# Finer handover steps for the attention units, other steps for the v_m products, and the order of their splits

## The chip, the cores and the metric

The program runs on one core of a Trainium2 chip. The metric is device time in microseconds (us) of one execution of the whole program. Before the change it is 1615.07 us, the median of 3 runs (1614.37 to 1615.68).

## The reference

Three stages follow each other. q, k, v have shape (8 batches, 8 heads, 576 positions, 64), phi (8, 8, 576, 32).

```python
a = exp(phi - max(phi));  a = a / (sum(a) + 1e-9)          # over the 32 memory slots
k_m = einsum('bhsm,bhsd->bhmd', a, k);  v_m = einsum('bhsm,bhsd->bhmd', a, v)
s = (q @ k_m.T) / sqrt(64);  p = softmax(s)                # 32 scores for each position
x = (p @ v_m), heads side by side                          # 4608 x 512
h = x @ w_in;  h = max(0.01 * h, h);  x = h @ w_out         # 512 -> 2048 -> 512
y = (sigmoid(x @ w_gate) * (x @ w_val)) @ w2_out            # 512 -> 1536 -> 512
```

## The kernel before, in words

**Precision.** Large products run on two float32r numbers for each float32: a high part (`hi`, a copy rounded on ScalarE) and a low part (`lo`, the rest, subtracted on VectorE or GpSimd). `split` (L157) makes both: L158 the copy, L159 the subtraction. A product takes three matmuls: hi by hi, lo by hi, hi by lo.

**The first network.** p @ v_m @ w_in is computed as p @ (v_m @ w_in). `vw_pair` (L717) makes v_m @ w_in of a batch for two of its 8 column blocks: 32 matmuls into two PSUM banks, one for each group of 4 heads, and then four `split`s, from the banks into two of the nine slots of the tag vw. So a batch needs four pairs. `m1_in` (L738) multiplies it with the attention weights p (`at_hi`, `at_lo`) and puts the leaky ReLU through ScalarE (gr) and a `split` (gh, gl); `m1_out` (L761) multiplies with w_out into four PSUM banks (acc), and at the end of a half batch copies acc to obuf (L781).

**Steps.** The main loop counts steps i. Step i runs `m1_out` of one block of 128 hidden columns and half a batch (288 positions); a batch has 32 steps, its first half in the first 16, and batch b from 1 on has steps 32b to 32b + 31. In the code of one step the order is: the split of gr that belongs to step i + 1 (`fin`), `m1_in` of step i + 2 with its gr, then vector work (`run(vs)`, the generators taking turns operation by operation), TensorE work of the units (`ts_`), `vw_pair` where its step has come, `m1_out`, and loads. Every engine takes its instructions in this order, and so a step that waits holds what stands behind it on its engine.

**Units.** The attention of one batch and one group of 4 heads is a unit, cut into parts (`PARTS`, L688): v1 to v11 on VectorE, ScalarE and GpSimd, t1 to t8 on TensorE, lp, lk, lq the loads. `SCHED["chain"]` gives each part its step, counted from the unit's own start; for batches 3 to 7 the two units start at step 32(b-1) - 8 and 32(b-1) + 8, for batches 1 and 2 at `units`. Parts that matter here: v5 (L521) takes reciprocals on VectorE and scales the new k_m, v_m on ScalarE out of PSUM (tile e, L541); t5, v6 make their transposes (kvT); t8, v8 the scores, two PSUM banks, transposed into e (L592) by VectorE; v9 (L633) the maximum on VectorE (L638) and the subtraction (L640), v9e exp on ScalarE (L647), v10 (L650) sum, reciprocal on VectorE (L654 to L658) and the product with it (L660), v10t (L665) a transpose on VectorE (L676), v11 (L679) the split into at_hi and at_lo. From batch 2 on the subtractions of v9 and v11 and the product of v10 are on GpSimd (POOL). t1, t2, t4, t5, t8 and the pairs share two PSUM buffers (`psa`, L432).

**The weights of the second network** are converted in the steps from 31 on, in 36 pieces (`stash_jobs`, L253), one stage of a piece in each step. A piece begins as float32 bits; stage a (L182) has three conversions on ScalarE (y L186, k L187, raw L189), b (L192) a clip on VectorE, b2 a combination of y and raw on VectorE, c an addition on GpSimd. Sums of the pieces are split (hl, L290 and L296) and stored to memory (gvs) for later. The pieces of a gate and value block begin at steps 0 and 3 of twelve, counted from step 31, and their splits are in steps 8 to 12 of the twelve; w2 pieces begin three steps apart.

**After step 255** comes the second network, matmuls on TensorE with operands from memory.

Of the kernel before, what the change touches and what calls it, by code (L numbers as in the profile page):

```python
# [8 lines left out]
F32 = mybir.dt.float32  # L9
# [5 lines left out]
AX = mybir.AxisListType  # L15
# [27 lines left out]
           'v4': 5,  # L43
           't4': 6,
           'vq': 6,
           'v5': 7,
           't5': 9,
           'v6': 10,
# [6 lines left out]
           'v11': 17},  # L55
 'units': [1, 13, 30, 42],
 'unit': [-8, 8],
 'vw': [20, 22, 36, 38],
 'vw_last': [20, 22, 25, 28],
 'vw1': [26, 28, 31, 37],  # L60
 'vw2': [54, 57, 59, 63],
 'groups': [4,4,4,4],
 'chain1': {'lp': -9,
            'lk': -4,
# [26 lines left out]
def tile_kernel(  # L91
# [13 lines left out]
    nc = tc.nc  # L105
    P = 128
    B, H, S, D = q.shape
# [13 lines left out]
    VB = 256  # L121
# [15 lines left out]
    q, k, v, phi = (x.rearrange("b (h g) s d -> b g h s d", g=NG) for x in (q, k, v, phi))  # L137
# [13 lines left out]
    def f32(ap):  # L151
        return ap.bitcast(F32)
# [4 lines left out]
    def split(raw, hi, lo, eng=nc.vector):  # L157
        nc.scalar.copy(hi, raw)  # L158
        eng.tensor_sub(lo, raw, f32(hi))  # L159
# [7 lines left out]
    PC = 512  # L167

    class Piece:
        i = -1  # L170

        def __init__(self, src, done, f_dst=None, raw=None):
            self.src, self.done, self.f_dst, self.raw = src, done, f_dst, raw
# [8 lines left out]
        def a(self):  # L182
            w = self.raw.rearrange("p (n t) -> p n t", t=2)
            self.y = cvp.tile([P, PC], F32, tag="y", name="y", bufs=5)
            self.k = cvp.tile([P, PC], F32, tag="k", name="k", bufs=4)
            nc.scalar.activation(self.y, w[:, :, 1].bitcast(F32), AF.Abs, scale=2.0 ** -3)  # L186
            nc.scalar.activation(self.k, w[:, :, 0], AF.Copy, scale=2.0 ** -27, bias=2.0 ** 25)  # L187
            hi = w[:, :, 1]
            nc.scalar.activation(hi.bitcast(I32), hi.bitcast(F32), AF.Prelu, scale=2.0 ** -60, alpha=2.0 ** 120)  # L189
            yield  # L190

        def b(self):  # L192
            y = self.y
            nc.vector.tensor_scalar(y, y, 2.0 ** -18, 15359.998046875, op0=ALU.max, op1=ALU.min)
            yield

        def b2(self):
# [55 lines left out]
    def stash_jobs():  # L253
        held = {}

        def conv(src, done):
            p = Piece(src, None)

            def c():
                yield from p.c()  # L260
                done(p.f)

            return p, [p.a, p.b, p.b2, c]
# [68 lines left out]
        for th in range(NTH):  # L332
            for j in range(TH // 2):
                for i, w in enumerate((w_gate, w_val)):
                    for e in range(2):
# [3 lines left out]
                            lambda f, k=((th, j, i), e): held.update({k: f}),  # L339
# [20 lines left out]
    vw = {}  # L360
    un = {}
# [67 lines left out]
    def unit_engine(part, u):  # L429
        return nc.gpsimd if u[0] > 1 or f"{part}.{u[0] * NG + u[1]}" in SCHED["upool"] else nc.vector  # L430
# [37 lines left out]
    def etile(u):  # L468
        if u == FIRST2:
            return un[u]["m0"][:, 0:S].rearrange("p (a m) -> p a m", m=M)  # L470
        return ap_.tile([P, S // 32, M], F32, tag="e", name="e")
# [46 lines left out]
                p[:, 4 * D:4 * D + 2], s["t"].rearrange("p h m -> p (h m)"), ones[:, 0:2], start=True, stop=True  # L518
            )

    def v5(u):  # L521
        s = un[u]
        p = s.pop("p")
        r = ap_.tile([P, 4], F32, tag="r", name="r", bufs=2)
        nc.vector.tensor_scalar_add(r[:, 0:1], p[:, 4 * D:4 * D + 1], 1e-9)
        yield
        nc.vector.reciprocal(r[:, 0:1], r[:, 0:1])
        yield
        if u[0] == 0:
            nc.vector.tensor_scalar_mul(r, mask, r[:, 0:1])  # L530
            yield
        x = etile(u)
        x = s["x"] = x.rearrange("p a m -> p (a m)")[:, 0:4 * D].rearrange("p (a f) -> p a f", a=2)
        if u[0] == 0:
            for j in range(2):
                nc.scalar.activation(x[:, 0, j * D:(j + 1) * D], p[:, 0:D], AF.Copy, scale=r[:, j:j + 1])
            for j in range(2):
                m = 2 if j == u[1] else 3
                nc.scalar.activation(x[:, 1, j * D:(j + 1) * D], p[:, D:2 * D], AF.Copy, scale=r[:, m:m + 1])
        else:  # L540
            nc.scalar.activation(  # L541
                x.rearrange("p i (a d) -> p i a d", a=2),
                p[:, 0:2 * D].rearrange("p (i a d) -> p i a d", i=2, a=1).to_broadcast([P, 2, 2, D]),
                AF.Copy, scale=r[:, 0:1],
            )
        yield

    def t5(u):
        s = un[u]
# [80 lines left out]
        )  # L630
        yield

    def v9(u):  # L633
        s = un[u]
        sc = s["sc"]
        nb = S // 32
        st = s["st"] = ap_.tile([P, nb], F32, tag="st", name="st", bufs=2)
        nc.vector.reduce_max(st, sc, axis=AX.X)  # L638
        yield
        unit_engine("v9", u).tensor_sub(  # L640
            sc, sc, st.rearrange("p (a o) -> p a o", o=1).to_broadcast([P, nb, M])
        )
        yield

    def v9e(u):
        sc = un[u]["sc"]
        nc.scalar.activation(sc, sc, AF.Exp, scale=SCALE)  # L647
        yield

    def v10(u):  # L650
        s = un[u]
        sc, st = s["sc"], s["st"]
        nb = S // 32
        nc.vector.reduce_sum(st, sc, axis=AX.X)  # L654
        yield
        nc.vector.tensor_scalar_add(st, st, 1e-9)
        yield
        nc.vector.reciprocal(st, st)  # L658
        yield
        unit_engine("v10", u).tensor_mul(  # L660
            sc, sc, st.rearrange("p (a o) -> p a o", o=1).to_broadcast([P, nb, M])
        )
        yield

    def v10t(u):  # L665
        s = un[u]
# [12 lines left out]
    def v11(u):  # L679
# [7 lines left out]

    PARTS = {  # L688
        "v1": v1, "t1": t1, "v2": v2, "t2": t2, "v3": v3, "v3e": v3e, "v4": v4, "t4": t4, "v5": v5, "t5": t5,
        "v6": v6, "v9": v9, "v9e": v9e, "v10": v10, "v10t": v10t, "v11": v11,  # L690
        "vq": vq, "t8": t8_both, "v8": v8_both, "lp": unit_phi, "lk": unit_kv,
    }
    for h in range(HG):
# [23 lines left out]
    def vw_pair(b, j0):  # L717
        js = (j0, j0 + 1)
        ps = [psa("ps_vw") for _ in range(NG)]
        for n, j in enumerate(js):  # L720
            for h in range(HG):
                for g in range(NG):
                    nc.tensor.matmul(  # L723
                        ps[g][M * h:M * h + M, n * VB:(n + 1) * VB],
                        kvT[b, g][D * g:D * g + D, 1, M * h:M * h + M],
                        win[j][D * g:D * g + D, h, :], start=True, stop=True,
                    )
        for j in js:
            vw[b, j] = wtile("vw", [P, 2, NG, VB], F32R, "vw")
        for g in range(NG):  # L730
            for n, j in enumerate(js):
                split(ps[g][:, n * VB:(n + 1) * VB], vw[b, j][:, 0, g], vw[b, j][:, 1, g])

    hps = {}
    gt = {}
# [289 lines left out]
    with tc.manual_schedule():  # L1025
# [91 lines left out]
        def unit_parts(i):  # L1117
            vs, ts_, ls = [], [], []
            for u, u0 in U0.items():
                parts = [n for n, k in SCHED["chain1" if u[0] == 1 else "chain"].items() if k == i - u0]  # L1120
                v = [PARTS[n](u) for n in parts if n[0] == "v"]
                if v:
                    vs.append(chain(v))
                ts_ += [(PARTS[n], u) for n in parts if n[0] == "t"]
                ls += [
                    (PARTS[n], u) for n in parts
                    if n[0] == "l" and u not in units[:3]
                ]
            return vs, ts_, ls
# [166 lines left out]
```

## Time and profile before

| what | value |
|---|---|
| median of 3 runs | 1615.07 us |
| the profiled execution: its own time, its span | 1615.78 us, 1614.0 us |
| mean granted TensorE clock | 0.989 of full speed |
| VectorE, ScalarE, GpSimd busy | 833.8, 710.8, 433.9 us (52%, 44%, 27% of the span) |
| matmul instructions | 10544 |
| memory read, written | 219.68 MB, 47.19 MB |

The span is from the first to the last instruction. A busy engine is one that executes; register, wait and DMA-issuing instructions don't count. Matmuls overlap each other, so that single times of matmuls add up to more than the time they take.

### The profile page before, as it was taken

The numbers are of one execution on the slowest core, as the hardware profiler recorded it, in microseconds if no ns is written. First come the engines' busy times: TensorE is split into PE (matmuls) and PEld (weight loads), VectorE is DVE, ScalarE is ACT, GpSimd is POOL, SyncE is SP. The second block draws the span as 40 slices with busy tenths as digits, with TensorE's granted clock in tenths as the row PEclk, the third lists the DMA queues.
The fourth block names the chain that finished last, engine by engine and source line by source line (L and its number), as shares of the span: only waits on it lengthen the run. The fifth ranks groups of instructions, "written<-read, shape, count | busy, mean of one in ns | idle before, by whom it ended". The sixth has DMA issues, their size and how long they took to land.

```text
span 1614.0 us, 27349 instructions
## 1 busy us (share of the span) xinstructions
PE 1553.8 (96%) x10544; PEld 1358.4 (84%) x10544; DVE 833.8 (52%) x1426; ACT 710.8 (44%) x1602; POOL 433.9 (27%) x429
## 2 busy tenths in 40 slices
PE   4789999999999999999999999999999999999998
PEld 2677888999898899999988888888888888888898
DVE  6986444455545445523154474365544474355544
ACT  5885455565556555645333142222333143223332
POOL 3886343554445444543200020000200020000100
PEclk9799999999999999999999999999999999999999
DMA  9822543554555554412455456546556446436592
GB/s 302 276 52 68 154 142 101 153 177 120 159 161 172 152 149 130 138 42 93 172 196 187 141 168 221 194 133 201 193 181 208 143 158 227 165 116 221 219 396 77
DMA packets 203490, 268.66 MB, mean 166 GB/s; under 512 B 95072, under 2 KB 140128, under 8 KB 203360
## 3 DMA queue, kind: packets, MB, share of 16 engines
q1 hardware_dynamic: 203360, 266.92, 51.5%
q8 instruction: 83, 1.36, 0.3%
q14 instruction: 47, 0.39, 0.1%
HBM read 219.68 MB, written 47.19 MB: 165 GB/s over the span
## 4 chain that ended last, share of the span: by engine, by line
PE 61%; DMA 1%; DVE 0%; ACT 0%; POOL 0%; issue 0%; SPq 0%
PE oacc L978 18%; PE ps_y L880 14%; PE ps_x L880 9%; PE ps_z L880 9%; PE acc L772 7%; PE ps_h L750 3%; DMA wt<-gvs 1%; PE ps_vw L723 0%; PE ps_kv L515 0%; ACT gh L158 0%; PE ps_sc L582 0%; POOL e L640 0%; DVE vw L159 0%; DVE sums L277 0%; DVE st L654 0%
## 5 line engine op out<-in xcount | busy, mean ns | idle before, releaser
L772 PE MATMUL acc<-gh,wo 128*128 128x288 f32 x2048 | 429.3, 301 | 7.1 <-ACT obuf L781 3.9
L772 PEld LDWEIGHTS acc<-gh,wo 128*128 128x128 f32 x2048 | 328.4, 189 | 33.6 <-issue 14.0
L772 PE MATMUL acc<-gl,wo 128*128 128x288 f32 x1024 | 306.2, 299 | 6.4 <-POOL gl L159 6.4
L159 POOL TENSOR_TENSOR gl<-gr,gh 128x288 fp32r<-128x288 f32 x250 | 216.4, 870 | 342.0 <-ACT gh L158 247.6
L978 PE MATMUL oacc<-w2t,pt 128*128 128x512 f32 x1296 | 296.3, 389 | 0.0
L978 PEld LDWEIGHTS oacc<-w2t,pt 128*128 128x128 f32 x1296 | 243.1, 188 | 50.4
L880 PE MATMUL ps_y<-xo,wt 128*128 128x512 f32 (+1 forms) x1080 | 251.9, 369 | 0.0
L750 PE MATMUL ps_h<-at_hi,vw 128*128 128x288 f32 x1024 | 215.3, 299 | 6.1 <-ACT vw L158 4.7
L880 PEld LDWEIGHTS ps_y<-xo,wt 128*128 128x128 f32 x1080 | 190.3, 188 | 33.8
L843 POOL TENSOR_TENSOR xo<-xr,xo 128x512 fp32r<-128x512 f32 (+1 forms) x16 | 23.0, 1460 | 671.0 <-ACT xo L839 671.0
L772 PEld LDWEIGHTS acc<-gl,wo 128*128 128x128 f32 x1024 | 193.7, 189 | 10.4 <-POOL gl L159 10.2
L755 ACT ACTIVATE gr<-ps_h 128x288 f32<-128x288 f32 x256 | 105.6, 413 | 204.4 <-PE ps_h L750 175.4
L750 PEld LDWEIGHTS ps_h<-at_hi,vw 128*128 128x128 f32 x1024 | 167.3, 191 | 7.5 <-ACT vw L158 5.6
L880 PE MATMUL ps_z<-xo,wt 128*128 128x512 f32 (+1 forms) x720 | 167.4, 368 | 0.9 <-DMA wt<-gvs 0.9
L880 PE MATMUL ps_x<-xo,wt 128*128 128x512 f32 (+1 forms) x720 | 167.5, 368 | 0.0
L750 PE MATMUL ps_h<-at_lo,vw 128*128 128x288 f32 x512 | 152.1, 297 | 0.0
L915 ACT CAST pt<-sg 128x512 fp32r<-128x512 f32 (+1 forms) x120 | 69.4, 578 | 182.0 <-DVE sg L908 182.0
L880 PEld LDWEIGHTS ps_z<-xo,wt 128*128 128x128 f32 x720 | 127.0, 188 | 23.5 <-DVE pt L912 1.1
L880 PEld LDWEIGHTS ps_x<-xo,wt 128*128 128x128 f32 x720 | 127.2, 188 | 22.9
L158 ACT CAST gh<-gr 128x288 fp32r<-128x288 f32 x256 | 111.3, 435 | 2.5
L750 PEld LDWEIGHTS ps_h<-at_lo,vw 128*128 128x128 f32 x512 | 97.6, 191 | 0.0
L927 ACT COPY tmp<-ps_x 128x512 f32<-128x512 f32 (+1 forms) x60 | 32.5, 542 | 136.7 <-PE ps_x L880 136.7
(169 smaller groups left out, 1730.4 us busy)
## 6 DMA issues: line engine op xcount, KB each, us to landing
wt<-gvs SPq DMA_DIRECT2D x210, 512.0 KB, 4.5
w2t<-w2s SPq DMA_DIRECT2D x60, 512.0 KB, 5.4
gvs<-hl SPq DMA_DIRECT2D x84, 256.0 KB, 2.3
x2s<-obuf SPq DMA_DIRECT2D x15, 576.0 KB, 3.7
win<-in_moe_w_in_dram SPq DMA_DIRECT2D x16, 512.0 KB, 9.8
wo_bits<-in_moe_w_out_dram SPq DMA_DIRECT2D x16, 512.0 KB, 10.3
xr<-x2s SPq DMA_DIRECT2D x16, 512.0 KB, 6.6
out_dram<-osum SPq DMA_DIRECT2D x32, 256.0 KB, 2.0
```

Of the source, the lines that this page charges most:

```text
L158: nc.scalar.copy(hi, raw)
L159: eng.tensor_sub(lo, raw, f32(hi))
L750: nc.tensor.matmul(p[:, :HALF], w, x, start=(n == 0), stop=(n == 3 * NG - 1))
L755: nc.scalar.activation(gr, p[:, :HALF], AF.Prelu, alpha=0.01)
L772: nc.tensor.matmul(a[d][:, :HALF], w[:, ds_], x, start=(open_ and n == 0), stop=(close and n == 2),)
L843: eng.tensor_sub(t[:, 1, :h], x_operand(n, k, a), f32(t[:, 0, :h]))
L880: nc.tensor.matmul(bank, w[:, l, a, :], x[:, r, :h], start=(start and i == 0), stop=(i == 5), skip_group_check=not start,)
L915: nc.scalar.copy(d[:, 0, :h], s)
L927: read(lambda: nc.scalar.copy(s1, x))
L978: nc.tensor.matmul(bank[i], pt[2 * f + t][:, l, q * P:(q + 1) * P], w2t[f][:, r, :], start=(f == 0 and l + r == 0), stop=(f == TH - 1 and ...
```

## The change

The chain that was used for batches 2 to 7 stays for batch 2 under the name `chain2`. The chain for batches 3 to 7 cuts v5, v9 and v10 where the work goes from one engine to another: v5r (reciprocals) and v5x (scaling) at 7 and 8 instead of both at 7; v9m (maximum), v9s (subtraction) and v9e (exp) at 13, 14, 15 instead of all at 13; v10r (sum and reciprocal) and v10m (product) at 16 and 17 instead of 14; v10t at 18 instead of 15, v11 at 20 instead of 17. The pairs of batches 3 to 6 go from steps 20, 22, 36, 38 (from 32(b-1)) to 21, 28, 32, 37, those of batch 7 each one step later, and the last of batch 2 from 63 to 64. In `vw_pair`, all pairs, the two high parts of a bank are written first and then its two low parts. For the 36 pieces converted from step 31 on (`late`) the third conversion goes from stage a to stage b, behind the clip. The instructions themselves and their operands stay.

```diff
--- before.py
+++ after.py
@@ -29,6 +29,34 @@
  'gldve': [3, 4, 6, 12, 26, 31],
  'upool': ['v10.1', 'v10.2', 'v10.3', 'v11.0', 'v11.1', 'v11.2', 'v11.3', 'v9.0', 'v9.2', 'v9.3'],
  'chain': {'lp': -8,
...
+           'v5r': 7,
+           'v5x': 8,
+           't5': 9,
+           'v6': 10,
+           't8': 11,
+           'v8': 12,
+           'v9m': 13,
+           'v9s': 14,
+           'v9e': 15,
+           'v10r': 16,
+           'v10m': 17,
+           'v10t': 18,
+           'v11': 20},
+ 'chain2': {'lp': -8,
            'lk': -5,
            'lq0': -8,
            'lq1': -7,
@@ -55,10 +83,10 @@
            'v11': 17},
  'units': [1, 13, 30, 42],
  'unit': [-8, 8],
- 'vw': [20, 22, 36, 38],
- 'vw_last': [20, 22, 25, 28],
+ 'vw': [21, 28, 32, 37],
+ 'vw_last': [21, 23, 26, 29],
  'vw1': [26, 28, 31, 37],
- 'vw2': [54, 57, 59, 63],
+ 'vw2': [54, 57, 59, 64],
  'groups': [4,4,4,4],
  'chain1': {'lp': -9,
             'lk': -4,
@@ -167,7 +195,7 @@
     PC = 512
 
     class Piece:
-        i = -1
+        late = False
 
         def __init__(self, src, done, f_dst=None, raw=None):
             self.src, self.done, self.f_dst, self.raw = src, done, f_dst, raw
@@ -185,13 +213,19 @@
             self.k = cvp.tile([P, PC], F32, tag="k", name="k", bufs=4)
             nc.scalar.activation(self.y, w[:, :, 1].bitcast(F32), AF.Abs, scale=2.0 ** -3)
             nc.scalar.activation(self.k, w[:, :, 0], AF.Copy, scale=2.0 ** -27, bias=2.0 ** 25)
-            hi = w[:, :, 1]
+            if not self.late:
+                self.sign()
+            yield
+
+        def sign(self):
+            hi = self.raw.rearrange("p (n t) -> p n t", t=2)[:, :, 1]
             nc.scalar.activation(hi.bitcast(I32), hi.bitcast(F32), AF.Prelu, scale=2.0 ** -60, alpha=2.0 ** 120)
-            yield
 
         def b(self):
             y = self.y
             nc.vector.tensor_scalar(y, y, 2.0 ** -18, 15359.998046875, op0=ALU.max, op1=ALU.min)
+            if self.late:
+                self.sign()
             yield
 
         def b2(self):
@@ -255,6 +289,7 @@
 
         def conv(src, done):
             p = Piece(src, None)
+            p.late = True
 
             def c():
                 yield from p.c()
@@ -518,10 +553,10 @@
                 p[:, 4 * D:4 * D + 2], s["t"].rearrange("p h m -> p (h m)"), ones[:, 0:2], start=True, stop=True
             )
 
-    def v5(u):
-        s = un[u]
-        p = s.pop("p")
-        r = ap_.tile([P, 4], F32, tag="r", name="r", bufs=2)
+    def v5r(u):
+        s = un[u]
+        p = s["p"]
+        r = s["r"] = ap_.tile([P, 4], F32, tag="r", name="r", bufs=2)
         nc.vector.tensor_scalar_add(r[:, 0:1], p[:, 4 * D:4 * D + 1], 1e-9)
         yield
         nc.vector.reciprocal(r[:, 0:1], r[:, 0:1])
@@ -529,6 +564,10 @@
         if u[0] == 0:
             nc.vector.tensor_scalar_mul(r, mask, r[:, 0:1])
             yield
+
+    def v5x(u):
+        s = un[u]
+        p, r = s.pop("p"), s["r"]
         x = etile(u)
         x = s["x"] = x.rearrange("p a m -> p (a m)")[:, 0:4 * D].rearrange("p (a f) -> p a f", a=2)
         if u[0] == 0:
@@ -545,6 +584,10 @@
             )
         yield
 
+    def v5(u):
+        yield from v5r(u)
+        yield from v5x(u)
+
     def t5(u):
         s = un[u]
         p = s["p"] = psa("ps_kvT")
@@ -630,37 +673,53 @@
         )
         yield
 
-    def v9(u):
-        s = un[u]
-        sc = s["sc"]
+    def v9m(u):
+        s = un[u]
         nb = S // 32
         st = s["st"] = ap_.tile([P, nb], F32, tag="st", name="st", bufs=2)
-        nc.vector.reduce_max(st, sc, axis=AX.X)
-        yield
+        nc.vector.reduce_max(st, s["sc"], axis=AX.X)
+        yield
+
+    def v9s(u):
+        s = un[u]
+        sc, st = s["sc"], s["st"]
+        nb = S // 32
         unit_engine("v9", u).tensor_sub(
             sc, sc, st.rearrange("p (a o) -> p a o", o=1).to_broadcast([P, nb, M])
         )
         yield
 
+    def v9(u):
+        yield from v9m(u)
+        yield from v9s(u)
+
     def v9e(u):
         sc = un[u]["sc"]
         nc.scalar.activation(sc, sc, AF.Exp, scale=SCALE)
         yield
 
-    def v10(u):
+    def v10r(u):
+        s = un[u]
+        sc, st = s["sc"], s["st"]
+        nc.vector.reduce_sum(st, sc, axis=AX.X)
+        yield
+        nc.vector.tensor_scalar_add(st, st, 1e-9)
+        yield
+        nc.vector.reciprocal(st, st)
+        yield
+
+    def v10m(u):
         s = un[u]
         sc, st = s["sc"], s["st"]
         nb = S // 32
-        nc.vector.reduce_sum(st, sc, axis=AX.X)
-        yield
-        nc.vector.tensor_scalar_add(st, st, 1e-9)
-        yield
-        nc.vector.reciprocal(st, st)
-        yield
         unit_engine("v10", u).tensor_mul(
             sc, sc, st.rearrange("p (a o) -> p a o", o=1).to_broadcast([P, nb, M])
         )
         yield
+
+    def v10(u):
+        yield from v10r(u)
+        yield from v10m(u)
 
     def v10t(u):
         s = un[u]
@@ -687,7 +746,8 @@
 
     PARTS = {
         "v1": v1, "t1": t1, "v2": v2, "t2": t2, "v3": v3, "v3e": v3e, "v4": v4, "t4": t4, "v5": v5, "t5": t5,
-        "v6": v6, "v9": v9, "v9e": v9e, "v10": v10, "v10t": v10t, "v11": v11,
+        "v5r": v5r, "v5x": v5x, "v6": v6, "v9": v9, "v9m": v9m, "v9s": v9s, "v9e": v9e, "v10": v10, "v10r": v10r,
+        "v10m": v10m, "v10t": v10t, "v11": v11,
         "vq": vq, "t8": t8_both, "v8": v8_both, "lp": unit_phi, "lk": unit_kv,
     }
     for h in range(HG):
@@ -728,8 +788,11 @@
         for j in js:
             vw[b, j] = wtile("vw", [P, 2, NG, VB], F32R, "vw")
         for g in range(NG):
-            for n, j in enumerate(js):
-                split(ps[g][:, n * VB:(n + 1) * VB], vw[b, j][:, 0, g], vw[b, j][:, 1, g])
+            ws = [(ps[g][:, n * VB:(n + 1) * VB], vw[b, j]) for n, j in enumerate(js)]
+            for x, w in ws:
+                nc.scalar.copy(w[:, 0, g], x)
+            for x, w in ws:
+                nc.vector.tensor_sub(w[:, 1, g], x, f32(w[:, 0, g]))
 
     hps = {}
     gt = {}
@@ -1117,7 +1180,7 @@
         def unit_parts(i):
             vs, ts_, ls = [], [], []
             for u, u0 in U0.items():
-                parts = [n for n, k in SCHED["chain1" if u[0] == 1 else "chain"].items() if k == i - u0]
+                parts = [n for n, k in SCHED[{1: "chain1", 2: "chain2"}.get(u[0], "chain")].items() if k == i - u0]
                 v = [PARTS[n](u) for n in parts if n[0] == "v"]
                 if v:
                     vs.append(chain(v))
```

## Rows read from the trace of the kernel before

**Rows 1.** The page, part 1: busy us, share, instructions.
```profile
PE 1553.8 (96%) x10544; PEld 1358.4 (84%) x10544; DVE 833.8 (52%) x1426; ACT 710.8 (44%) x1602; POOL 433.9 (27%) x429
```

**Rows 2.** Stretches of undisturbed steps: from:to, us, busy by engine, clock, DMA.
```profile
721.47:791.07 69.60, 69.60 (x525) 69.60 (x523) 16.20 (x22) 31.75 (x77) 27.13 (x30) 1.00 0.38 131
274.42:277.57 3.15, 3.15 (x36) 2.52 (x35) 1.54 (x2) 1.31 (x4) 0.81 (x1) 1.00 0.88 232
371.59:375.09 3.50, 3.50 (x52) 2.80 (x50) 2.89 (x5) 1.54 (x5) 2.11 (x2) 1.00 0.46 123
```

**Rows 3.** Stretches of two steps, where v9 to v10t end.
```profile
280.07:286.03 5.96, 5.38 (x39) 4.90 (x37) 2.27 (x4) 3.44 (x8) 3.23 (x4) 1.00 1.02 320
...
655.43:661.03 5.60, 5.34 (x40) 5.03 (x39) 3.27 (x7) 4.25 (x11) 3.99 (x6) 1.00 0.56 187
```

**Rows 4.** Waits of TensorE, 266 to 715 us: total us, times, longest.
```profile
PE acc L772 <- POOL gl L159: 3.9, 10, 0.5
PE acc L772 <- ACT obuf L781: 2.0, 4, 0.7
PE ps_vw L723 <- DVE e L592: 1.7, 4, 0.6
PE acc L772 <- ACT gh L158: 1.4, 4, 0.7
```

**Rows 5.** Stretches of one step at the end of a half.
```profile
266.41:269.34 2.93, 2.70 (x25) 2.46 (x19) 1.50 (x4) 1.75 (x6) 0.00 (x0) 1.00 0.02 6
...
584.53:587.84 3.31, 2.57 (x20) 2.34 (x18) 0.73 (x2) 2.77 (x7) 0.00 (x0) 1.00 0.20 77
```

**Rows 6.** Order of time, ScalarE at step 127: start, us, instruction.
```profile
446.53 0.47 ACT L541 ACTIVATE e<-ps_kv,r 128x256 f32<-128x256 f32 x1
...
448.55 1.30 ACT L781 COPY obuf<-acc 128x288 f32<-128x288 f32 x4
```

**Rows 7.** Stretches of one step, a pair in the step of v8.
```profile
409.89:414.61 4.72, 4.24 (x58) 3.05 (x51) 2.26 (x6) 2.83 (x7) 0.81 (x1) 1.00 0.88 272
...
548.40:553.49 5.09, 4.32 (x58) 3.06 (x51) 2.26 (x6) 3.22 (x8) 0.81 (x1) 1.00 0.89 281
```

**Rows 8.** Stretches of one step, a pair in the step of v5.
```profile
179.31:183.92 4.61, 4.23 (x54) 3.06 (x50) 1.54 (x4) 0.78 (x2) 1.79 (x2) 1.00 0.27 46
261.81:266.41 4.60, 4.22 (x55) 3.04 (x51) 1.15 (x4) 1.07 (x3) 0.54 (x1) 1.00 0.00 0
```

**Rows 9.** Stretches of step 31, of step 57 and the one after.
```profile
163.60:168.14 4.54, 3.10 (x28) 2.73 (x21) 2.11 (x6) 3.47 (x10) 0.50 (x1) 1.00 0.01 4
235.47:244.84 9.37, 5.26 (x53) 3.24 (x51) 5.15 (x11) 3.83 (x8) 4.35 (x5) 0.87 0.18 61
244.84:249.42 4.58, 4.58 (x28) 4.58 (x21) 1.61 (x4) 1.73 (x5) 1.54 (x2) 0.52 0.32 108
```

**Rows 10.** Order of time, all engines at step 57; the idle time before in brackets.
```profile
239.46 0.41 ACT L158 CAST gh<-gr 128x288 fp32r<-128x288 f32 x1
...
240.75 1.16 POOL L660 TENSOR_TENSOR e<-e,st 128x576 f32<-128x576 f32 x1
...
242.95 1.96 PE L723 MATMUL ps_vw<-win,kvT 64*32 64x256 f32 x30 [4.11 <-DVE mx L457]
```

**Rows 11.** Order of time, ScalarE at step 163.
```profile
549.20 0.41 ACT L290 CAST hl<-sums 128x256 fp32r<-128x256 f32 x1 [2.97 <-DMA gvs<-hl]
```

**Rows 12.** Order of time, ScalarE: the copies of a pair.
```profile
415.57 0.36 ACT L158 CAST vw<-ps_vw 128x256 fp32r<-128x256 f32 x1
...
416.42 0.65 ACT L158 CAST vw<-ps_vw 128x256 fp32r<-128x256 f32 x2 [0.49 <-DVE vw L159]
...
417.62 0.37 ACT L158 CAST vw<-ps_vw 128x256 fp32r<-128x256 f32 x1 [0.55 <-DVE vw L159]
```

**Rows 13.** The tile raw: duration in ns (min/median/max), first and last start.
```profile
L189 ACT ACTIVATE raw<-raw x36: 648/669/701, 164.2 to 678.8; 128x512 int32<-128x512 f32 x36
```

**Rows 14.** A stretch after the gap of step 57.
```profile
243.00:249.00 6.00, 6.00 (x47) 4.78 (x48) 2.30 (x6) 1.73 (x5) 1.12 (x2) 0.50 0.28 87
```

More of the change, by code (lines that the diff above doesn't have):

```diff
@@ L45 @@
            'vq': 6,
+           'v5r': 7,
[12 more added lines that the diff above has]
+ 'chain2': {'lp': -8,
+           'lk': -5,
+           'lq0': -8,
+           'lq1': -7,
+           'lq2': -4,
+           'lq3': -3,
+           'v1': -5,
+           't1': 0,
+           'v2': 1,
+           't2': 2,
+           'v3': 3,
+           'v3e': 4,
+           'v4': 5,
+           't4': 6,
+           'vq': 6,
            'v5': 7,
@@ L648, in v9e @@
         yield
-    def v10(u):
+    def v10r(u):
         s = un[u]
         sc, st = s["sc"], s["st"]
-        nb = S // 32
         nc.vector.reduce_sum(st, sc, axis=AX.X)
@@ L659, in v10 @@
         yield
+    def v10m(u):
+        s = un[u]
+        sc, st = s["sc"], s["st"]
+        nb = S // 32
         unit_engine("v10", u).tensor_mul(
```

## Prediction

> **What bounds the kernel now.** I read the page's totals first, then stretches of the trace laid on single steps, then the waits of TensorE, then the order of time on ScalarE, VectorE and GpSimd around each stall. TensorE is busy in 96% of the span [rows 1]. So a gain in the middle can only come from gaps between matmuls. Where no attention unit is in work, 29 steps take 69.60 us, 2.40 us each, and TensorE has no gap [rows 2]; that is the floor of a step. An undisturbed step with the score products takes 3.15 us, one with a pair of v_m products 3.50 [rows 2]. From 721 us (step 224) on nothing is changed, and the second network behind it is TensorE's too. What can move is the excess over these floors in steps 25 to 221.
>
> I found it by comparing every step with its floor. It falls into kinds:
> - **A, POOL chain.** Every 16 steps, where v9 to v10t of a unit end, two neighbouring steps are late. Nine such pairs of steps; the first has 5.96 us, the last 5.60 [rows 3], against 4.80 for two plain steps (4.90 where a small transposition is in one): 1.16 and 0.70 lost, over all nine 9.8 us. What ends the wait on TensorE is gl from POOL and gh from ACT [rows 4]: POOL's product of v10 stands in its queue until its sums are through DVE, and gl stands behind it.
> - **B, the end of a half batch.** Steps 63, 79, 127 and 175, the first with 2.93 and the last with 3.31 us instead of 2.40 [rows 5]: 2.7 us in the four. The next half's first matmul waits for the ACT copy acc to obuf [rows 4]. In ACT's order v5's scaling and the three conversions of a piece stand before that copy: the four take from 446.53 to 448.55, half a us each [rows 6].
> - **C, a pair in the step of v8.** Steps 116, 148 and 164, the first with 4.72 and the last with 5.09 us instead of 3.50 [rows 7]: 3.8 us in the three, because both PSUM buffers still hold scores that DVE transposes out (ps_vw waits for DVE e [rows 4]).
> - **D, a pair in the step of v5.** 4.61 and 4.60 us [rows 8], 1.1 each.
> - **E, step 31 (4.54 us) and step 57 (9.37, and 4.58 in the next)** [rows 9]. At 57 the pair waits 4.11 us for DVE mx [rows 10], which stands behind a transpose that needs POOL's v10 product.
>
> **The change, part by part.**
>
> *Chain of batches 3 to 7.* v9 and v10 are cut so that each engine's part is issued a step after its input. No instruction is added, DMAs stay at their steps, and v10t and v11 go 3 steps later (v11 of the second unit at step 28 of 32; its reader is issued at 30). POOL's product is then ready when it reaches the head of the queue and takes 1.16 us [rows 10] beside gl. This removes A: -9.8 us at most. v5x goes from the closing step to the one after it, out of the way of obuf: it and the moved conversion (below) free obuf about 1.0 us earlier than in [rows 6], more than the 0.91 lost at step 175. This removes B: -2.7 at most.
>
> *Pairs at 21, 28, 32, 37.* The first goes one step past v8: C goes, -3.8 at most. The second (28) meets v3e and v11 on ACT, about 4 us of work in a 3.5 us step; the next thing that TensorE needs from there is due two steps later, so I take nothing. Bounds: 0 to the 0.7 us that the longest gh wait has [rows 4], five times. The third (32) now stands in the step of v5x, at steps 96, 128, 160, 192; it stood at 36, free of waits. That is kind D again: its second matmul needs the bank that v5x reads, and in ACT's queue v5x stands behind four obuf copies (1.30 us [rows 6]), gh and gr. Queued behind the waiting matmul is all of TensorE. By [rows 8] 1.1 us each; at step 128 I take 1.5, since two conversions and the obuf copies go ahead of it. Sum +4.8; bounds 0 and four times the 4.11 us of [rows 10]. Batch 2's last pair goes from 63 to 64 and takes its 1.1 along: 0.
>
> A fifth of A, B and C I leave standing, since ACT also stalls on buffers that the change doesn't touch: up to 2.97 us for a store of hl [rows 11]. So -16.3 x 0.8 = -13.0.
>
> *High parts first in vw_pair.* ACT and DVE each issue the same instructions in the same order as before; only what they wait for can change. Before, the second copy of a bank starts 0.49 us after the first ended, released by DVE's subtraction of the first [rows 12]: reads of one bank by ACT and DVE are taken in turns. ACT is held from 415.57 to 417.99 by four copies of which two back to back take 0.65 us [rows 12]; in the new order they take about 1.3 us, 1.1 us less, and the first bank is free some 0.6 us earlier. Bounds: nothing (if the turns stay), to 1.1 us for each of 28 pairs where ACT is what TensorE waits for, which [rows 4] shows only in the stalls above. I count it where a stall hangs on it: step 31, where t2 waits for the bank and the next half for pbuf behind the subtractions, -1.3 us of its excess of 2.0.
> The Trainium skill (PSUM — Partial Sum Buffer, "PSUM bank collisions raise a hardware error") says that the compiler orders any two accesses of one bank from different engines, reads too. The wait of 0.49 us agrees. By it the first subtraction will now wait for the second copy, which puts off its start by 0.3 us and changes no term of the sum; without it DVE would finish that much earlier.
>
> *`late`: the third conversion one step later.* 36 instructions of 0.67 us [rows 13], each now behind the next step's gr instead of ahead of the next gh. Cover: gh has a step in hand. Bounds: 36 x 0.5 = 18 us of ACT either way if ACT were the bound; it is not, so I take 0 beside its share in B and E, and 0.3 us at step 45 (a stall on gl behind the three conversions).
>
> *Step 57.* Its unit of batch 2 keeps the old chain, so the wait stays. But what leads to it gets shorter: the pair of step 54 frees DVE and ACT about 0.7 us earlier for v9, and gh, which starts at 239.46 [rows 10] behind the three conversions, has one less in front (0.5). POOL's product starts at 240.75 right behind that gl [rows 10]. So mx comes 1.2 us earlier and the gap is 2.9 us instead of 4.11: -1.2. In the gap the granted clock falls from 1.00 to 0.50, that is from 2.4 to 1.2 GHz, and stays there through 243 to 249 [rows 14]. The two stretches of [rows 9] together lose 7.9 us over their floors (3.55 and 2.5); less the gap that is 3.8 us. In the busy stretch before it TensorE had no gap of this size, so I expect the shorter one to pass at 2.4 GHz: -3.8.
> The Trainium skill (TensorE: Matmul & The Clock Gate, "What's actually happening") says the array's clock halves when it was idle long enough, and that its windows run free of the kernel. By that whether 2.9 us is short enough depends on where it falls; this trace shows one such gap in the steady part, with the clock lost; the time would be the forecast's or rival 1's.
>
> Sum: -13.0 + 4.8 - 1.3 - 0.3 - 1.2 - 3.8 = -14.8 us. On the profiled execution, 1615.78 us (span 1614.0 and 1.8 around it, 0.7 above the median of the runs), 1601.0; against the median 1615.07, **1600.3 us**.
>
> **The rivals.**
> 1. *The clock still falls at step 57.* Everything else as above: 1600.3 + 3.8 = 1604.1 us. For it: the gap is long against all others in the steady part (0.7 us at most [rows 4]). Against it: the gap shrinks by a quarter.
> 2. *The stalls change their name.* POOL and ACT do the same work; a chain spread over 3 more steps meets other pieces' conversions, and of A, B and C only 4.8 us go, which the four new waits take back. With no gain at 57: about 1614 to 1616 us. For it: ACT's waits for stores [rows 11]. Against it: A recurs at the same place of the chain in nine of nine, so it belongs to the chain.
> 3. *Slower: the pair at 32.* If ACT is held ahead of v5x by a store as in [rows 11] (2.97 us), the pair's matmul waits over 4 us, the clock falls, and each of the four costs 7.9 us as step 57 does instead of 1.2: 1600.3 + 4 x 6.7 = 1627 us. It decides from three of the four on (20 us against 14.8). Against it: the copies into hl stand after v5x in that step's order, and of the steps before it only 159 has one (its step is undisturbed in the trace of before).
> 4. *The new order does nothing* because both queues keep theirs: then -1.3 and some 0.6 of the 1.2 at 57 are gone, and the clock with them: 1606 us. This is inside rival 1's chance.
>
> **How the numbers follow.** Forecast 0.55; the clock or the order (rivals 1, 4) 0.27; no change 0.08; slower 0.10. A difference under 0.2% (3.2 us) can't be told from none here. Faster 0.82, within 0.08, slower 0.10. Around the forecast: none to two fifths of A, B, C left is -3.3 to +3.3; the pairs at 32 for nothing -4.8, at twice the price +4.8. Low end: 1600.3 - 3.3 - 4 = 1593. High end: rival 1's 1604.1 with two fifths left (+3.3) and the pairs somewhat dearer (+2.5): 1610. That leaves out rivals 2 and 3 and little else.
>
> **What would show it.** Right: no waits of acc for POOL gl around steps 88, 104, ... ; the steps 79, 127, 175 at 2.4 us; pairs at 85, 117, 149, 181 at 3.5; steps 96, 128, 160, 192 at 4.6 to 5.0 with the wait on ACT e; ACT's copies of a bank back to back; a gap of about 3 us at step 57 and clock 1.00 after it. Wrong: waits of several us at the pairs of 32, a clock below 1.00 there, or stalls on gl that stay while POOL has no v10 product before them.

## The result and the profile after

The changed kernel takes 1600.43 us (median of 4 runs, 1599.10 to 1601.75), the one before, run beside it, 1615.35: a ratio of 0.9906, with a 95% interval of 0.9894 to 0.9918. The profiled execution took 1601.75 us with a span of 1599.9 us.

The page, part 1 (busy us, share of the span, instructions). The instructions are as many as before. Of the 14.1 us by which the span is shorter, TensorE's idle time gives 9.4 and its busy time 4.7:

```profile
PE 1549.1 (97%) x10544; PEld 1358.0 (85%) x10544; DVE 827.7 (52%) x1426; ACT 707.9 (44%) x1602; POOL 431.0 (27%) x429
```

All waits of TensorE in the part that is [rows 4] before, 252 to 702 us here (total us, times, longest). The four kinds of before are gone, gl, obuf, e from v8 and gh; two others stand there, both 0 in [rows 4]. Of the five waits for ACT e one is not new: batch 2's pair, which had it at 63, just ahead of that part, and has it at 64 now (0.4 us).

```profile
PE ps_vw L783 <- ACT e L580: 2.8, 5, 1.2
PE ps_kv L541 <- DVE t L532: 2.1, 3, 1.0
```

Stretches of the changed kernel that answer to rows of before (from:to, us, busy by engine, clock, DMA):

```profile
707.91:777.51 69.60, 69.60 (x525) 69.60 (x523) 16.33 (x22) 31.76 (x77) 26.35 (x30) 1.00 0.38 131
274.90:279.70 4.80, 4.80 (x39) 4.80 (x38) 0.69 (x1) 2.12 (x5) 2.09 (x3) 1.00 1.09 255
642.48:647.49 5.01, 5.01 (x41) 5.01 (x39) 2.77 (x6) 2.37 (x6) 4.16 (x5) 1.00 0.41 130
572.08:574.49 2.41, 2.41 (x20) 2.41 (x19) 0.43 (x1) 2.15 (x6) 0.00 (x0) 1.00 0.18 68
540.01:542.52 2.51, 2.51 (x26) 2.51 (x19) 1.94 (x4) 1.49 (x3) 0.79 (x2) 1.00 1.05 368
163.31:166.44 3.13, 2.87 (x28) 2.70 (x21) 1.93 (x6) 2.44 (x9) 0.81 (x1) 1.00 0.00 0
233.22:240.90 7.68, 4.60 (x54) 3.02 (x51) 4.47 (x9) 3.61 (x8) 3.67 (x4) 0.94 0.19 70
240.90:244.66 3.76, 3.76 (x26) 3.76 (x21) 1.42 (x4) 1.53 (x5) 2.00 (x2) 0.66 0.43 139
348.24:352.74 4.50, 4.11 (x52) 2.94 (x50) 0.69 (x1) 3.17 (x9) 0.79 (x1) 1.00 0.19 68
437.78:443.14 5.36, 4.14 (x52) 2.96 (x51) 0.43 (x1) 4.32 (x11) 0.98 (x2) 1.00 0.44 157
340.67:345.72 5.05, 4.09 (x69) 3.49 (x67) 4.96 (x9) 3.54 (x10) 2.57 (x3) 1.00 0.18 67
```

In order: 29 undisturbed steps, the same to a hundredth as in [rows 2], so that 13.6 of the 14.1 us lie ahead of them; the other 0.5 arise after step 253, where nothing was changed. Then the first and last of the nine double steps with v9 to v10t (4.80 and 5.01 instead of 5.96 and 5.60 [rows 3]), step 175 (2.41 instead of 3.31 [rows 5]), the step of v8 that the pair has left (2.51 [rows 7]; the pair is in the next, 3.50), step 31 and step 57 with its neighbour [rows 9]. The last three are new losses: the pair in the step of v5x at 96 and 128, and step 94, whose floor with the key-value product t4 is 3.90.

The copies and subtractions of a pair, ScalarE and VectorE in order of time:

```profile
230.13 1.19 ACT L793 CAST vw<-ps_vw 128x256 fp32r<-128x256 f32 x4
...
230.80 1.42 DVE L795 TENSOR_TENSOR vw<-ps_vw,vw 128x256 fp32r<-128x256 f32 x4 [1.98 <-ACT vw L793]
```

Four copies hold ScalarE for 1.19 us without a wait, where they were spread over 2.4 [rows 12]. VectorE starts 0.67 us after ScalarE, behind two copies, as the turns on a bank want it; that is the 0.3 us behind the first copy's end that I had reckoned with.

### The profile page after: what moved, and what is told of

Read it like the earlier page. It is cut to its first block, busy times and chain, and to the rows that moved or that the text cites. A ratio compares the mean times of both kernels' runs of the same rounds, so it can differ in the third digit from the quotient of the medians.

```text
span 1599.9 us, 27447 instructions
## 1 busy us (share of the span) xinstructions
PE 1549.1 (97%) x10544; PEld 1358.0 (85%) x10544; DVE 827.7 (52%) x1426; ACT 707.9 (44%) x1602; POOL 431.0 (27%) x429
## 4 chain that ended last, share of the span: by engine, by line
PE 82%; ACT 1%; DVE 1%; DMA 1%; issue 0%; POOL 0%; DVEq 0%; SPq 0%; ACTq 0%; POOLq 0%
PE acc L835 20%; PE oacc L1041 18%; PE ps_y L943 14%; PE ps_h L813 9%; PE ps_x L943 9%; PE ps_z L943 9%; PE ps_vw L783 1%; PE ps_kv L550 1%; DMA wt<-gvs 1%; PE ps_sc L625 0%; ACT gr L818 0%; ACT obuf L844 0%; DVE vw L795 0%; DVE t L530 0%; ACT raw L222 0%
```

## The experiments

The first four make one part of the change in the kernel before.

**Chain alone.** The diff's `chain` and its functions; in `SCHED`:

```diff
- 'vw2': [54, 57, 59, 63],
+ 'vw2': [54, 57, 59, 64],
```

> The kernel before with the finer chain alone: v5, v9, v10 cut by engine for batches 3 to 7. Batch 2's last pair goes to step 64, since at 63 it would stand ahead of the v5x that it waits for; all other pairs, the order of the copies and the three conversions stay as before. My theory (the waits on gl and gh every 16 steps are POOL's and ACT's queues held by a chain within one step): all nine of them go, about -9.8 us, of the half-batch ends about half (v5 leaves, three conversions stay, -1.4), pairs in the step of v8 stay: 1604 us. Rival (these waits come from ScalarE being held by the alternating copies of the pairs): less than half of them goes, 1610 us or more.

1605.71 us, ratio 0.9942 (0.9929 to 0.9954). Waits of TensorE from 252 to 715 us:

```profile
PE ps_vw L783 <- DVE e L635: 1.1, 3, 0.5
PE acc L832 <- POOL gl L187: 0.8, 2, 0.4
PE ps_vw L783 <- ACT e L580: 0.4, 1, 0.4
PE ps_kv L541 <- DVE t L532: 0.2, 1, 0.2
```

Ten waits on gl [rows 4] have become two, at steps 105 and 201, and obuf is gone. The nine double steps take 46.0 us together instead of 53.7, so that A loses 7.7 us and not 9.8: seven of the nine are cleared, the two with these waits are not (5.89 and 5.85 us, before 5.65 and 5.60). Mostly as my theory had it, 1.7 us short of it.

**Order of the copies alone.** In `vw_pair`:

```diff
-            for n, j in enumerate(js):
-                split(ps[g][:, n * VB:(n + 1) * VB], vw[b, j][:, 0, g], vw[b, j][:, 1, g])
+            ws = [(ps[g][:, n * VB:(n + 1) * VB], vw[b, j]) for n, j in enumerate(js)]
+            for x, w in ws:
+                nc.scalar.copy(w[:, 0, g], x)
+            for x, w in ws:
+                nc.vector.tensor_sub(w[:, 1, g], x, f32(w[:, 0, g]))
```

> The kernel before with the two high parts of a bank first in all pairs, and nothing else. My theory: ScalarE and VectorE take turns on a bank, so four copies run back to back (1.2 us from first to last instead of 2.4); it pays at step 31 (-0.9 us of 4.54) and at step 57 (gap 3.4 us instead of 4.11, the clock falls all the same, -0.7 to -1.5), and little elsewhere: 1612 to 1613 us. Rival (the queues keep their order, so nothing changes): copies still alternate, 1615 us.

1602.31 us, ratio 0.9923 (0.9909 to 0.9937): 10 us better than I thought. The waits, same view:

```profile
PE ps_vw L723 <- DVE e L592: 1.6, 3, 0.6
PE acc L775 <- ACT obuf L784: 1.4, 3, 0.5
PE ps_vw L723 <- ACT e L541: 0.4, 1, 0.4
```

No wait on gl or gh is left, though the chain is the old one. The nine double steps take 44.5 us together instead of 53.7. So what made gl late was on ScalarE; the trace of before shows it too (in the part on the prediction).

**The pairs' steps alone.**

```diff
- 'vw': [20, 22, 36, 38],
- 'vw_last': [20, 22, 25, 28],
+ 'vw': [21, 28, 32, 37],
+ 'vw_last': [21, 23, 26, 29],
- 'vw2': [54, 57, 59, 63],
+ 'vw2': [54, 57, 59, 64],
```

> The kernel before with the pairs of batches 2 to 7 at the changed steps, and nothing else. Here v5 stays at 31 of 32, so the third pair at 32 comes a step after it. My theory: the waits of pairs for v8's transposes go (-3.8), the pair of batch 2 loses its wait for v5 (-1.1), steps 96, 128, 160, 192 show no wait of the pair for ScalarE, and the new waits of the key-value product for VectorE (0.4 to 1.0 us at steps 94, 126, 190 of the changed kernel) come with the pair at 28: +2.6; 1612 us, the waits on gl stay. Rival (the wait at 32 belongs to the half-batch's end, not to v5x): these four steps still take 4.5 us or more, 1616 us.

1611.86 us, ratio 0.9983 (0.9974 to 0.9992), as expected. Waits, same view:

```profile
PE acc L772 <- POOL gl L159: 2.6, 6, 0.6
PE ps_kv L506 <- DVE t L497: 2.6, 4, 1.0
PE acc L772 <- ACT obuf L781: 1.0, 2, 0.5
PE acc L772 <- ACT gh L158: 0.6, 1, 0.6
```

No wait of the pair for ACT e: with v5 at step 31 the pair at 32 is undisturbed. The wait of the changed kernel is v5x's. The key-value product's new wait is there without the chain, so it is the pairs'.

**The moved conversion alone.**

```diff
             p = Piece(src, None)
+            p.late = True
```

> The kernel before with the third conversion of the 36 pieces one step later, and nothing else. My theory: half a us less of ScalarE ahead of what stands behind it in the step where a piece begins: step 31 -0.5, step 45 -0.5, half-batch ends 79, 127, 175 -0.5 each, step 57 a gap 0.5 us shorter: 1611 to 1612 us. Rival (the conversion only moves its delay to the next step): 1614 us or more, as many stalls at other steps.

1609.93 us, ratio 0.9969 (0.9956 to 0.9981), 1 to 2 us better than expected. Steps 31 and 45 lose 0.6 us each of their time, 79 to 81 0.57, and of the nine double steps the first (5.96 to 5.10), while the waits on gl fall only from ten to eight:

```profile
PE acc L832 <- POOL gl L187: 2.9, 8, 0.4
```

The four alone save 9.4, 12.4, 2.7 and 5.0 us (1 minus the ratio, of 1615): 30 us, where together they save 15. The next three take one part out of the changed kernel. The moved conversion was not taken out, so what it is worth beside the rest is open.

**Without the order of the copies.** `vw_pair` as before, the rest as changed.

```diff
-            for x, w in ws:
-                nc.scalar.copy(w[:, 0, g], x)
-            for x, w in ws:
-                nc.vector.tensor_sub(w[:, 1, g], x, f32(w[:, 0, g]))
+            for n, j in enumerate(js):
+                split(ps[g][:, n * VB:(n + 1) * VB], vw[b, j][:, 0, g], vw[b, j][:, 1, g])
```

> The changed kernel with the copies and subtractions of a pair in the old order, the rest of the change kept. The copies alone made 1602.3 us and the chain alone 1605.7. Theory R (the stalls every 16 steps need two causes at once, ScalarE held by alternating copies and a chain within one step, so that either edit clears them): they stay gone here too, and only step 31 (+0.5), step 57 (+0.5 to +2.5) and the waits of the key-value product and of the third pair grow a little: 1602 to 1605 us. Rival S (the copies do the work, the chain adds only the half-batch ends): the stalls on gl come back, 1610 us.

1608.94 us, ratio 0.9960 (0.9947 to 0.9972). All its waits, same view:

```profile
PE ps_kv L541 <- DVE t L532: 5.8, 4, 2.2
PE ps_vw L783 <- ACT e L580: 2.4, 5, 0.9
```

No wait on gl or gh is back, as theory R has it. That the chain alone does this is not shown: by itself it left two waits on gl, behind an exp and three conversions on ScalarE, and this kernel keeps the moved conversion and the pairs' steps beside the chain. In the time I missed by 4 us, because the key-value product's wait grows to 2.2 us: the slower subtractions of the pair at 28 stand longer ahead of v4 on VectorE.

**Without the pairs' steps.** `vw` and `vw_last` as before.

```diff
- 'vw': [21, 28, 32, 37],
- 'vw_last': [21, 23, 26, 29],
+ 'vw': [20, 22, 36, 38],
+ 'vw_last': [20, 22, 25, 28],
```

> The changed kernel with the pairs of batches 3 to 7 back at 20, 22, 36, 38 (20, 22, 25, 28 in the last batch); batch 2's last pair stays at 64. By the step tables so far: the waits of the pair for ScalarE's e at 96, 128, 160, 192 go (-5.2), those of the key-value product go (-2.6), the pairs in the step of v8 wait again (+3.8), nothing else: 1596 to 1597 us, so the moved pairs cost more than they bring. Rival (the old steps bring back stalls behind the pair at 22 or 38): 1600 us or more.

1597.21 us, ratio 0.9891 (0.9878 to 0.9905), as worked out: the moved pairs cost about 3 us by the medians once the rest is there.

**Without the chain.**

```diff
- parts = [n for n, k in SCHED[{1: "chain1", 2: "chain2"}.get(u[0], "chain")].items() if k == i - u0]
+ parts = [n for n, k in SCHED["chain1" if u[0] == 1 else "chain2"].items() if k == i - u0]
```

> The changed kernel with the old chain for batches 3 to 7, so copies, the moved conversion and the pairs' steps alone. If the chain's gain is already in the copies' order, and the finer chain is what makes the pair at 32 wait (v5x in its step): steps 96, 128, 160, 192 at 3.6 us without that wait (-4.9), batch 2's pair at 64 without it too (-1.0), half-batch ends 79, 127, 175 partly back (+1.0): 1595 to 1596 us. Rival (without the finer chain the stalls on gl come back, as POOL still holds gl behind v10's product): 1602 us or more.

1595.75 us, ratio 0.9882 (0.9867 to 0.9898). Step 96 is at its floor, where the changed kernel has 4.50:

```profile
345.55:349.04 3.49, 3.49 (x52) 2.79 (x50) 0.69 (x1) 3.16 (x9) 0.26 (x1) 1.00 0.01 4
```

The nine double steps take 46.0 us instead of 44.2; two waits on gl are back, at 120 and 201:

```profile
PE acc L835 <- POOL gl L187: 0.9, 2, 0.7
PE ps_kv L541 <- DVE t L532: 0.7, 2, 0.4
```

So with the copies in their new order the finer chain, the change's largest part, saves 1.8 us of A and 0.2 at each of two ends of a half. It costs more: the waits of the pair (4.9 us in four steps, 1.0 at step 64) and 1.6 us at the key-value product, whose waits fall from 2.1 to 0.7 us without it. That is 4.7 us by the medians, and 4.9 by the two traces from step 59 to 224. The last ones change the changed kernel further.

**Third pair later.**

```diff
- 'vw': [21, 28, 32, 37],
+ 'vw': [21, 28, 37, 39],
```

> The changed kernel with the pairs of batches 3 to 6 at 21, 28, 37, 39 instead of 21, 28, 32, 37: the third no longer in the step of v5x. My theory: the four waits of the pair for ScalarE's e (0.4 to 1.2 us each, steps 4.5 to 5.4 us instead of 3.5) go and nothing takes their place: -5.2 us, 1595 us. Rival (two pairs two steps apart load ScalarE and VectorE so that the wait returns at v9 to v11 or at the next score product): 1599 us or more.

1602.61 us, ratio 0.9922 (0.9911 to 0.9934). My theory fell. Steps 96, 128, 160 and 192 are at their floor, but steps 102 and 103 (362.50 to 372.57 us) take 10.1 us, where two plain steps and a pair would be 5.9, and 196 to 202 lose likewise. ScalarE and TensorE there:

```profile
365.05 0.40 ACT L325 CAST hl<-y 128x256 fp32r<-128x256 f32 x1 [2.71 <-DMA gvs<-hl]
365.36 1.19 ACT L793 CAST vw<-ps_vw 128x256 fp32r<-128x256 f32 x4
```

```profile
365.78 0.40 PE L813 MATMUL ps_h<-at_hi,vw 128*128 128x288 f32 x1 [1.44 <-ACT vw L793]
366.51 0.40 PE L813 MATMUL ps_h<-at_hi,vw 128*128 128x288 f32 x1 [0.33 <-DVE vw L795]
```

The pair at 37 is needed one step later. Here ScalarE stands 2.71 us behind a store of hl ahead of its copies, and `m1_in` waits for them. At 32 there were six steps of slack; the wait for v5x was their price.

**Second pair earlier.**

```diff
- 'vw': [21, 28, 32, 37],
+ 'vw': [21, 23, 32, 37],
```

> The changed kernel with the pairs of batches 3 to 6 at 21, 23, 32, 37 instead of 21, 28, 32, 37. My theory: the new waits of the key-value product for VectorE t (0.95, 0.73, 0.42 us at steps 94, 126, 190) stem from the subtractions of the pair at 28 ahead of v4 on VectorE: they go, -2.6 us, 1598 us. Rival (they stem from v3e and v4 themselves, or from ScalarE waiting for stores): the waits stay, 1600 us.

1599.42 us, ratio 0.9903 (0.9890 to 0.9915). Against the changed kernel the times alone can't tell it from none; the trace can: the wait on t is gone, step 94 is at its floor, and steps 59 to 224 take 2.4 us less.

```profile
338.93:342.86 3.93, 3.93 (x68) 3.37 (x67) 3.58 (x5) 2.75 (x8) 3.68 (x4) 1.00 0.46 156
```

**v10t of one unit a step later** (batch 2's second unit, at 58).

```diff
- parts = [n for n, k in SCHED[...].items() if k == i - u0]
+ parts = [n for n, k in SCHED[...].items() if k + (u == (2, 1) and n == "v10t") == i - u0]
```

> The changed kernel with one part of one unit, v10t of batch 2's second unit, at step 58 instead of 57, so that the maximum which the pair of step 57 waits for no longer stands behind it on VectorE. My theory: the gap at 57 shrinks from 3.08 us to 1 us or less, the granted clock stays at 1.00, steps 57 and 58 take about 7 us in place of 11.4: -4.5 us, 1596 us. Rival (VectorE is late at 57 for its whole chain): the gap only falls to 2 us or more, 1599 us.

1597.23 us, ratio 0.9889 (0.9877 to 0.9902). Steps 57 and 58, without a gap and at full clock:

```profile
234.07:237.65 3.58, 3.58 (x53) 2.88 (x50) 2.35 (x7) 3.58 (x8) 1.33 (x2) 1.00 0.34 126
237.65:240.56 2.91, 2.91 (x28) 2.70 (x21) 2.91 (x6) 1.66 (x7) 2.89 (x4) 1.00 0.18 39
```

6.49 us instead of 11.44. VectorE's order, one transpose ahead of one maximum, was the whole of that gap. By the medians it is 3.2 us: what step 57 costs the changed kernel differs from execution to execution, as shown below.

**Together, third pair at 37.**

```diff
- 'vw': [21, 28, 32, 37],
+ 'vw': [21, 23, 37, 39],
- 'vw2': [54, 57, 59, 64],
+ 'vw2': [54, 57, 59, 69],
```
and v10t as above.

> The changed kernel with the three edits together: pairs of batches 3 to 6 at 21, 23, 37, 39, batch 2's last pair at 69 instead of 64 (out of the step of v5x, another -1.0), v10t of batch 2's second unit at 58. My theory (the stalls are independent of each other): -5.2 - 2.6 - 1.0 - 4.5 = -13.3, 1587 us. Rival (they share ScalarE and VectorE, so that one grows when another goes): 1592 us or more.

1596.02 us, ratio 0.9881 (0.9868 to 0.9894). Not independent: against the next kernel, which has no pair at 39, steps 99 to 106 and 195 to 202 take 2.6 and 3.2 us more, of which the pair itself is 1.1 each.

**Together, third pair at 29.**

```diff
- 'vw': [21, 23, 37, 39],
+ 'vw': [21, 23, 29, 37],
```

> The changed kernel with the pairs of batches 3 to 6 at 21, 23, 29, 37, batch 2's last pair at 69, and v10t of batch 2's second unit at 58. Two pairs at 37 and 39 cost about 5.5 us at each of steps 99 to 106 and 195 to 202, where ScalarE's copies for the stored weights wait for stores. My theory: at 29 the third pair meets neither v5x nor those copies, v4 stands ahead of its subtractions, and the third pair costs its 1.1 us and no more: 1590 us. Rival (at 29 its subtractions hold the bank that the key-value product of step 30 needs, so the waits at 94, 126, 190 are back or larger): 1594 us or more.

1592.46 us (1591.91 to 1592.75), ratio 0.9860 (0.9847 to 0.9874), the fastest here; its interval lies below that of the changed kernel. One kind of wait is left from 252 to 715 us:

```profile
PE acc L835 <- POOL gl L187: 0.8, 2, 0.4
```

It is 2.5 us over my 1590. The rival's wait at 94, 126, 190 didn't come back; these two waits on gl, at 199 and 201, did.

## Why the prediction was right

The sum was 14.8 us off the profiled execution; it fell from 1615.78 to 1601.75, by 14.0. By terms, from the same stretches:

| term | predicted | measured |
|---|---|---|
| A, nine double steps | -9.8, of which four fifths | 53.7 to 44.2: -9.5 |
| C, pair in the step of v8 | -3.8, of which four fifths | three steps and the next: -3.5 |
| B, ends of a half | -2.7, of which four fifths | no wait on obuf left; 63 and 64 -0.5, 79 to 81 -0.75, 175 to 177 -1.02 |
| pair in the step of v5x, four times | +4.8 | 1.00, 1.86, 1.01, 0.99 over 3.50: +4.9 |
| key-value product | 0 | 1.15, 0.87, 0.60 over 3.90: +2.6 |
| step 31; step 45 | -1.3; -0.3 | -1.4; -0.6 |
| step 57 and the next | -5.0 | -2.5 |

The measured terms come to -12.3. Of the other 1.7 us, 0.3 lie ahead of step 24 and 0.5 behind step 253, where the change touches nothing; the rest is in steps that the table leaves out.

**Right:** the floor and the kinds of excess, that the change's gain lies between steps 31 and 202 (13.2 of the 14.0 us), and the price of the pair at 32, which I took from the two steps of [rows 8]. Step 128, with two conversions ahead, was dearer as said, 1.9 us instead of the 1.5 taken. Rivals 2 and 3 did not come: A, B and C are nearly gone, and the pair's four waits are 0.4 to 1.2 us, at full clock.

**Right in the sum by luck: sizes that cancel.** The fifth of A, B and C kept standing (3.3 us) was not kept: those stalls went nearly altogether, and these terms gave 2.3 us more than forecast, steps 31 and 45 another 0.4. With the 1.7 us that no term had, this makes up, but for 0.8 us, for what came out worse: step 57 by 2.5 us and the pair at 28, which I had set to nothing and which cost 2.6. I had looked for its cost on ScalarE and gh. The path is one engine further:

```profile
340.12 1.14 ACT L793 CAST vw<-ps_vw 128x256 fp32r<-128x256 f32 x4
340.76 1.42 DVE L795 TENSOR_TENSOR vw<-ps_vw,vw 128x256 fp32r<-128x256 f32 x4 [4.42 <-ACT vw L793]
342.10 1.08 DVE L530 TENSOR_REDUCE t<-e 128x128 f32<-128x512 f32 x1
343.78 0.27 DVE L532 TENSOR_TENSOR t<-t,pht 64x128 f32<-64x128 f32 x1
...
344.20 0.24 PE L541 MATMUL ps_kv<-ones,t 128*32 128x2 f32 x8 [0.95 <-DVE t L532]
```

At step 94, then: v3e, v11 and two conversions hold ScalarE, the pair's copies come late, VectorE's subtractions wait 4.42 us for them, and v4 stands behind, for which t4 waits 0.95 us.

**Wrong in the cause of A.** I gave its 9.8 us to the chain, because POOL's product of v10 would keep gl waiting, and to the copies' order only 1.3 at step 31 ("I count it where a stall hangs on it"). That step of the prediction failed: the copies alone save 12.4 us, over 9 of them in A. The trace of before had it already. ScalarE and POOL at step 120:

```profile
420.86 0.69 ACT L647 ACTIVATE e<-e 128x576 f32<-128x576 f32 x1 [2.22 <-POOL e L640]
...
424.02 1.18 POOL L660 TENSOR_TENSOR e<-e,st 128x576 f32<-128x576 f32 x1
...
425.80 0.37 ACT L158 CAST vw<-ps_vw 128x256 fp32r<-128x256 f32 x1 [0.55 <-DVE vw L159]
426.07 0.43 ACT L158 CAST gh<-gr 128x288 fp32r<-128x288 f32 x1
426.64 1.75 POOL L159 TENSOR_TENSOR gl<-gr,gh 128x288 fp32r<-128x288 f32 x2 [1.44 <-ACT gh L158]
```

POOL has ended its product at 425.20 and then stands idle for 1.44 us, until gh. And gh stands on ScalarE behind an exp that waited 2.22 us for POOL's subtraction, three conversions and the pair's four alternating copies, the last of them at 425.80. None of the ten gl of [rows 4] starts right behind a product of v10: where one goes before, it ended at least 1.1 us earlier. In eight of the ten the four copies are the last thing ahead of gh on ScalarE. I had held that A belongs to the chain since it recurs every 16 steps; the pairs at 22 and 38 do so too.

So, as far as these runs show, two causes on ScalarE add up: the pair's copies, which hold it for 2.4 us or more, and the exp of the chain, which waits for another engine. The copies' new order clears A alone, the chain alone clears seven of nine double steps; with the chain taken out of the changed kernel two waits on gl come back, and the one at 120 then does stand right behind v10's product, as I had pictured it. The order of the copies is worth 8.5 us where the rest is in place (1608.94 against 1600.43), now mostly at the key-value product, and the finer chain costs more than it brings beside the rest (1595.75 without it). Step 31 was right in size only: of its 1.4 us the copies alone make 0.85 and the moved conversion alone 0.62. My rival 4, that the new order does nothing, is refuted by the copies in the profile after.

**Step 57: the gap right, the clock wrong.** I had 2.9 us of gap; the profiled one is 3.08:

```profile
239.47 1.50 PE L783 MATMUL ps_vw<-win,kvT 64*32 64x256 f32 x30 [3.08 <-DVE mx L492]
```

Behind it the granted clock is at 0.50, which is 1.2 GHz:

```profile
240.90:243.20 2.30, 2.30 (x14) 2.30 (x10) 1.42 (x4) 1.53 (x5) 0.55 (x1) 0.50 0.70 228
```

So rival 1 came true in this term. But the gap is not the same in every execution. In the kernel with the second pair earlier, whose code is the changed kernel's up to here, it was 1.78 us, the clock stayed, and steps 57 and 58 took 8.6 us instead of 11.4:

```profile
234.29:240.27 5.98, 4.20 (x53) 3.02 (x51) 3.19 (x8) 3.35 (x8) 2.67 (x3) 1.00 0.16 60
```

TensorE is 1.0 us later in that profile from step 24 on (142.89 and 143.88 us), and still is three steps ahead of the gap, where ScalarE waits for a store of hl. ScalarE in the changed kernel, and then in the other:

```profile
227.95 0.40 ACT L325 CAST hl<-y 128x256 fp32r<-128x256 f32 x1 [3.10 <-DMA gvs<-hl]
```

```profile
227.75 0.41 ACT L325 CAST hl<-y 128x256 fp32r<-128x256 f32 x1 [1.78 <-DMA gvs<-hl]
```

TensorE in the same two, at the same step:

```profile
228.23 0.54 PE L835 MATMUL acc<-gh,wo 128*128 128x288 f32 x2
```

```profile
229.33 0.53 PE L835 MATMUL acc<-gh,wo 128*128 128x288 f32 x2
```

The store frees ScalarE at nearly the same time in both, and 11.5 us later mx ends the wait in both (239.47 and 239.25). TensorE is 1.1 us later in the second, and so it waits 1.3 us less at 57. Steps 57 and 58 differ by 2.8 us, but 1.1 of them were lost before: behind step 58 the two profiles are 1.8 us apart (244.66 and 242.90). The changed kernel's four runs stand at 1599.1, 1599.2, 1601.7 and 1601.8 us; that these are the two outcomes was not shown, since only one of the four has a profile.

## What to carry to other kernels

Edits that clear the same marginal stall don't add up, and a stall is named after the engine that is last, not after the one that made it late: before crediting an edit, ask which of the others would clear the same wait alone, and look what the engine named was itself waiting for. When work is moved to another step, list on every engine what is emitted behind it in that step, two engines down the chain, and how many steps its reader leaves it. Where two engines read one PSUM bank, give each its accesses in one run.

## What the runs showed of the hardware

- ScalarE and VectorE read one PSUM bank in turns even where their data don't depend on each other: 0.49 us from the end of a copy to the next, ended by VectorE's subtraction [rows 12], and none when the copies come first.
- Gaps of TensorE at step 57 and the clock behind them, one profile for each kernel: with 4.11 us (before), 3.08 (changed) and 2.46 (without the pairs' steps, where the stretch with the gap has 0.87) the clock fell, as with the 3.23 to 4.12 of five other kernels here; with 1.99 (without the chain), 1.95 (third pair later) and 1.78 (second pair earlier) it stayed at 1.00. I had hoped that a gap of 2.9 us would pass.
- Executions of the same code differ in time: TensorE began step 54 at 228.23 us in the changed kernel and at 229.33 in the one with the second pair earlier, which has the same code up to there, while ScalarE came free of the store 0.2 us apart. The gap at step 57 was 1.3 us longer where TensorE came early, and the clock behind it cost 1.5 more.
